# Output and down weights loaded in 4096-byte runs and put in row order on the chip, with a shorter root and a split silu

## The chip, the cores and the metric

The kernel runs on one core of a Trainium2 chip. The metric is the device time of one execution in microseconds (us). The engines are TensorE (PE; its weight loads are a row of their own, PEld), VectorE (DVE), ScalarE (ACT), GpSimd (POOL) and SyncE (SP), which here only issues transfers. Sixteen DMA engines move data between the chip's main memory and the on-chip memory SBUF (128 partitions); TensorE writes its sums to PSUM, eight banks of 512 f32 values in each partition.

## The reference

Two layers, each an attention block over a cached K and V and then a two-matrix silu block, for eight sequences of one token. The second layer uses the same caches and weights as the first.

```python
B, D = 8, 512;  Hq, Hkv, Sk, Dh = 32, 8, 8192, 128;  F = 1792      # all bf16
def A(x):                        # x: 8 x 512, after layernorm
    q = x @ wq                   # 512 x 4096
    p = softmax(q . K / sqrt(128))         # four query heads share one K/V head
    return (p . V) @ wo                    # wo: 4096 x 512
def Bl(x):
    return silu(x @ w1) @ w2               # w1: 512 x 1792, w2: 1792 x 512
for _ in range(2):
    x = x + A(layernorm(x))
    x = x + Bl(layernorm(x))
```

K and V are 8 x 8 x 8192 x 128 each, 134 MB each; the weights are 4.19 MB (wq), 4.19 MB (wo), 1.84 MB (w1) and 1.84 MB (w2).

## The kernel before

The unit of work is a chunk: 2048 keys of one sequence and one K/V head, 512 KB of K and 512 KB of V. Four chunks make a task (one sequence, one head, one layer), and there are 128 tasks. An arena of 28 slots of 512 KB in SBUF (`ARENA`, `NSLOT`) holds chunks. A planner (`lay_loads`, line 184) gives every load its slot, and the point at which that slot is free; `issue_until` (444) issues the loads in the planner's order on SP's queue as the program passes these points, so that SP waits in order for whoever last used the slot. The tasks are ordered so that parts of K and V read for the first layer are still in SBUF for the second.

For a chunk, TensorE transposes K in 16 blocks of 128x128 (line 479), ScalarE and VectorE copy the halves back from PSUM (485, 487), TensorE forms the scores with four 32-column tiles side by side (505), and six chunks later multiplies V by the probabilities (565). The softmax of a task is spread over VectorE, GpSimd and ScalarE (514 to 554). `LAG` is 6 chunks, `AHEAD` is 8.

When all heads of a sequence are through the first layer, its rest follows as a chain of small steps put between the chunks (`chain_of`, 715): the sum over wo (683, called from `add_heads`, 807), layernorm (`ln_stages`, 582, with the reciprocal root of line 632 on: a bit shift for a first guess, then two refinements), w1, tanh for silu, w2, layernorm, and the queries of the second layer. After the last task `closing` (776) does the end of the second layer for all eight sequences at once: layernorm, w1, silu (792 to 797) and w2 (799).

The start is written out by hand. SP issues eight K loads (456), then wq (449), then the first loads of all other slots (459), then wo, w1 and w2 (452 to 454). In wo_sb, partition p holds rows p, 128 + p, 256 + p and so on, so each piece that is read is one row of 512 values, 1024 bytes; w2 is the same, w1 is read in pieces of 3584 bytes, and a K or V load in pieces of 4096 bytes (8192 where two chunks go together). TensorE transposes the eight K chunks (840), multiplies by wq (843), and VectorE copies the queries to `QA` (844). Then the loop over the chunks begins (878).

Of the kernel before, what the change touches and what calls it, by code (L numbers as in the profile page):

```python
# [22 lines left out]
NTP = 3  # L23
# [215 lines left out]
def _build(ctx, nc, A_x, A_k_cache, A_v_cache, A_wq, A_wo, B_w1, B_w2, out):  # L239
# [50 lines left out]
    w1_sb = sb([128, KT, F], BF16, "w1")  # L290
    w2_sb = sb([128, FT, D], BF16, "w2")
    ident = sb([128, 128], BF16, "ident")
    XA = sb([128, 3, KT, B], BF16, "XA")
    XT = [XA[:, n] for n in range(3)]
    NT = 4
# [53 lines left out]

    syn = Sync(nc, ctx)  # L350
    slsem = [DmaCounter(syn.new_sem(f"sl{i}")) for i in range(NSLOT)]
    wsem = {n: DmaCounter(syn.new_sem(f"w_{n}")) for n in ("wq", "wo", "w1", "w2", "x")}
    osem = syn.new_sem("osem")

    R = {}
# [54 lines left out]
    with nc.Block() as block:  # L410

        @block.sync
        def _(sync_eng):
            dma(act, Xr[0:B, :], x_in, wsem["x"], writes=["P"])

            op(pool, lambda: pool.memset(ident[:, :], 0.0), writes=["ident"])
            along, down_ = QA[:, 0, :], QA[:, 1, :]
            op(dve, lambda: dve.memset(along[:, 0:1], 0.0), writes=["QA0"])
            n = 1
            while n < QR:  # L420
                op(dve, lambda n=n: dve.tensor_scalar(along[:, n:2 * n], along[:, 0:n], float(n), None, op0=ALU.add),
                   reads=["QA0"], writes=["QA0"])
                n *= 2
            op(dve, lambda: dve.transpose(down_, along), reads=["QA0"], writes=["QA1"])
            for t in range(NT):
                at = slice(t * QR, (t + 1) * QR)
                op(dve, lambda at=at: dve.tensor_tensor(ident[at, at], along[at, :], down_[at, :], ALU.is_equal),
                   reads=["QA0", "QA1", "ident"], writes=["ident"])
# [32 lines left out]

            evacs = [0]

# [118 lines left out]
            def ln_stages(xv, rx, n, bufs):  # L582
# [48 lines left out]

                def third():
                    vi, yi = v.bitcast(INT32), y.bitcast(INT32)
                    op(dve, lambda: dve.tensor_scalar(v, s1a[:, 0:n], 1.0 / D, LN_EPS, op0=ALU.mult, op1=ALU.add),
                       reads=["s1a"], writes=["vr"])
                    op(dve, lambda: dve.tensor_scalar(yi, vi, 1, None, op0=ALU.logical_shift_right),
                       reads=["vr"], writes=["yr"])
                    op(dve, lambda: dve.tensor_scalar(yi, yi, -1.0, RSQRT_SEED, op0=ALU.mult, op1=ALU.add),
                       reads=["yr"], writes=["yr"])
                    op(dve, lambda: dve.tensor_scalar(v, v, -0.5, None, op0=ALU.mult), reads=["vr"], writes=["vr"])  # L640
                    near(RSQRT_STEPS[0])

                def fourth():
# [20 lines left out]
            def wo_part(g, rhs_of, r_rhs, n, first, last):  # L664
                steps = []
                for o in range(KT):
                    for h in range(g * REP, (g + 1) * REP):
                        steps.append(
                            lambda o=o, h=h: pe.matmul(
                                MISC[:, o * n:(o + 1) * n], wo_sb[:, h, o * 128:(o + 1) * 128], rhs_of(h),  # L670
                                start=first and o == 0 and h == g * REP, stop=last and h == (g + 1) * REP - 1,
                                skip_group_check=True,
                            )
                        )
                mm_group(steps, reads=["wo"] + r_rhs, writes=["MISC"])

            def spread(col):
                return col.to_broadcast([128, QR])
# [36 lines left out]
            def chain_of(b):  # L715
# [21 lines left out]
                def down(q0, q1):  # L737
                    def run():
                        tiles([(t, hsT[:, q:q + 1], across(w2_sb[:, q, :], 0, KT)[:, t], q == 0, q == FT - 1)
                               for q in range(q0, q1) for t in range(NT)], ["w2", "hsT"])  # L740
                    return run

                AC = KB // QR
# [32 lines left out]
            def closing(n):  # L776
                xc, _sq, xn, _tag = ends
                memset = op(pool, lambda: pool.memset(ones, 1.0), writes=[r_half(spare, 0), r_half(spare, 1), "ones"])
                for r in ("xc8", "sq8", "xn8", "eh8", "th8", "hs8", "XF", "XO"):
                    syn.release(memset, writes=[res(r)])  # L780

                def rest():
                    x0, x1 = XT[2], XT[1]
                    add_residual(x1, "XT1", x0, "XT2", n)
                    centre, spread_of, guess, root = ln_stages(x1, "XT1", n, ends)
                    centre()
                    op(act, lambda: act.copy(xn, xc), reads=["xc8"], writes=["xn8"])
                    project(w1_sb, "w1", FT, KT, lambda k: xn[:, k, :], "xn8", n)
                    spread_of()
                    guess()  # L790
                    root()
                    op(dve, lambda: dve.scalar_tensor_tensor(
                        ehN.rearrange("p (f b) -> p f b", b=n), MISC[:, 0:FT * n].rearrange("p (f b) -> p f b", b=n), 0.5,
                        yr[:, 0:n].unsqueeze(1).to_broadcast([128, FT, n]), op0=ALU.mult, op1=ALU.mult),
                       reads=["MISC", "yr"], writes=["eh8"])
                    op(act, lambda: act.activation(thN, ehN, ACT.Tanh), reads=["eh8"], writes=["th8"])
                    op(dve, lambda: dve.scalar_tensor_tensor(hsN, thN, 1.0, ehN, op0=ALU.add, op1=ALU.mult),
                       reads=["th8", "eh8"], writes=["hs8"])
# [8 lines left out]
            def add_heads(b):  # L807
# [3 lines left out]
                if b < B:  # L811
                    a = at1[b % 3]
                    tiles([(t, a[:, h:h + 1], across(wo_sb[:, h, :], 0, KT)[:, t], first and h == g * REP,
                            last and h == (g + 1) * REP - 1)
                           for h in range(g * REP, (g + 1) * REP) for t in range(NT)], ["wo", f"at1_{b % 3}"])
# [28 lines left out]
            op(  # L844
                dve,
                lambda: dve.tensor_copy(
                    QA[:, :, :].rearrange("p b h -> p h b"),
                    MISC[:, 0:HQ * B].rearrange("p (h b) -> p h b", b=B)),
                reads=["MISC"], writes=[f"QA{b}" for b in range(B)],
            )  # L850

            emit_q(0)
# [106 lines left out]
```

## Time and profile before

| | |
|---|---|
| time, median of 3 runs | 1151.31 us (1146.54 to 1153.69) |
| profiled execution, its own time | 1151.22 us |
| its span, first to last instruction | 1149.4 us |
| mean granted TensorE clock | 0.910 |
| bytes by DMA | 459.43 MB in 100333 packets |
| wo, from issue to landing | 29.3 us |
| wq, from issue to landing | 19.7 us |

The profile gives for each engine its busy time, and for a stretch of time the busy time of each engine with its count of instructions, the granted TensorE clock (1.00 is full speed), the mean busy share of the DMA engines and GB/s. The share goes over 1 where packets overlap, so the GB/s say more than the share. A timeline row has start, length, engine, line, operation, what it writes and reads, its shapes and, in brackets, how long the engine stood idle before it and who ended that. A wait is given to the one that came last. The chain that ended last is followed back from the last instruction, at each step to what released it.

### The profile page before, as it was taken

The numbers are of one execution on the slowest core, as the hardware profiler recorded it, in microseconds if no ns is written. First come the engines' busy times: TensorE is split into PE (matmuls) and PEld (weight loads), VectorE is DVE, ScalarE is ACT, GpSimd is POOL, SyncE is SP. The second block draws the span as 40 slices with busy tenths as digits, with TensorE's granted clock in tenths as the row PEclk, the third lists the DMA queues.
The fourth block names the chain that finished last, engine by engine and source line by source line (L and its number), as shares of the span: only waits on it lengthen the run. The fifth ranks groups of instructions, "written<-read, shape, count | busy, mean of one in ns | idle before, by whom it ended". The sixth has DMA issues, their size and how long they took to land.

```text
span 1149.4 us, 42541 instructions
## 1 busy us (share of the span) xinstructions
PE 930.6 (81%) x18616; PEld 698.0 (61%) x18616; DVE 538.5 (47%) x1713; ACT 471.5 (41%) x747; POOL 117.6 (10%) x299
## 2 busy tenths in 40 slices
PE   5568888888888887888888887888878888888786
PEld 4356664666566664766566655666566655666565
DVE  3334453445534553446434553446434553456333
ACT  3235442455325541454235542554245432554332
POOL 0000011001110101001110111001100111011110
PEclk8689997899879997999789996999789996999897
DMA  9999999999999999999999999999999999999994
GB/s 371 393 396 414 383 386 412 418 411 387 406 418 416 394 402 419 418 410 393 400 418 416 389 407 417 419 404 378 413 419 414 390 410 417 417 400 399 404 418 190
DMA packets 100333, 459.43 MB, mean 400 GB/s; under 512 B 10540, under 2 KB 16436, under 8 KB 73780
## 3 DMA queue, kind: packets, MB, share of 16 engines
q1 hardware_dynamic: 100132, 456.70, 99.0%
q8 instruction: 147, 2.41, 0.9%
q14 instruction: 38, 0.31, 0.1%
q10 hardware_dynamic: 16, 0.01, 0.0%
HBM read 456.66 MB, written 0.01 MB: 397 GB/s over the span
## 4 chain that ended last, share of the span: by engine, by line
DMA 55%; PE 28%; DVE 10%; SPq 3%; issue 3%; ACT 0%; POOL 0%; POOLq 0%; ACTq 0%; DVEq 0%
DMA arena<-in_A_v_cache_dram 43%; PE TPp L479 15%; DMA arena<-in_A_k_cache_dram 10%; DVE arena L487 8%; PE SCp L505 6%; PE OTp L565 4%; SPq L379 3%; DMA wo<-in_A_wo_dram 3%; PE MISC L683 2%; PE TPp L545 1%; DVE small L554 0%; DVE small L535 0%; DVE small L525 0%; PE MISC L655 0%; ACT P L529 0%
## 5 line engine op out<-in xcount | busy, mean ns | idle before, releaser
L485 ACT COPY arena<-TPp 128x1024 bf16<-128x1024 bf16 x352 | 356.2, 1012 | 434.1 <-PE TPp L479 431.6
L487 DVE COPY arena<-TPp 128x1024 bf16<-128x1024 bf16 x352 | 243.4, 692 | 367.5 <-PE TPp L479 364.7
L479 PE MATMUL TPp<-ident,arena 128*128 128x128 bf16 x5632 | 391.6, 225 | 23.6 <-DMA arena<-in_A_k_cache_dram 20.9
L479 PEld LDWEIGHTS TPp<-ident,arena 128*128 128x128 bf16 x5632 | 330.0, 100 | 118.8 <-DMA arena<-in_A_k_cache_dram 65.9
L565 PE MATMUL OTp<-PT,arena 128*128 128x32 bf16 x8192 | 292.7, 179 | 74.7 <-DMA arena<-in_A_v_cache_dram 71.5
L565 PEld LDWEIGHTS OTp<-PT,arena 128*128 128x128 bf16 x8192 | 251.9, 98 | 158.9 <-DMA arena<-in_A_v_cache_dram 132.5
L505 PE MATMUL SCp<-arena,QB 128*32 128x512 bf16 x2048 | 223.9, 429 | 76.7 <-DVE arena L487 24.9
L529 ACT ACTIVATE P<-SCp,small 128x512 bf16<-128x512 f32 x128 | 88.0, 687 | 206.5 <-DVE small L527 148.6
L516 DVE TENSOR_REDUCE small<-SCp 128x1 f32<-128x512 f32 x128 | 88.5, 691 | 109.5 <-PE SCp L505 108.4
L505 PEld LDWEIGHTS SCp<-arena,QB 128*32 128x32 bf16 x2048 | 61.4, 97 | 118.3 <-ACT arena L485 64.8
L520 POOL PARTITION_ALL_REDUCE small<-small x128 | 47.6, 372 | 607.1 <-DVE small L518 607.1
L537 POOL PARTITION_ALL_REDUCE small<-small x128 | 55.4, 433 | 356.6 <-DVE at L579 160.9
L545 PE MATMUL TPp<-ident,P 128*128 128x128 bf16 x512 | 55.2, 237 | 11.5 <-ACT P L529 11.0
L535 DVE TENSOR_SCALAR small<-small 128x4 f32<-128x4 f32 x128 | 28.6, 223 | 37.9 <-ACT P L529 37.9
L549 DVE COPY PT<-TPp 128x256 bf16<-128x256 bf16 x128 | 36.7, 287 | 10.9 <-PE TPp L545 9.1
L545 PEld LDWEIGHTS TPp<-ident,P 128*128 128x128 bf16 x512 | 32.7, 103 | 14.7 <-ACT P L529 14.5
L683 PE MATMUL MISC<-wo,at 128*32 128x128 bf16 x1024 | 27.2, 239 | 13.1 <-DMA wo<-in_A_wo_dram 13.1
L518 DVE TENSOR_SCALAR small<-small 128x4 f32<-128x4 f32 x128 | 29.4, 229 | 4.5
L525 DVE TENSOR_TENSOR small<-small 128x4 f32<-128x4 f32 x128 | 19.9, 156 | 20.9 <-POOL small L520 20.9
L696 DVE STREAM_TRANSPOSE UP<-MISC 128x128 f32<-128x128 f32 (+2 forms) x40 | 22.1, 552 | 15.3 <-PE MISC L683 15.3
L683 PEld LDWEIGHTS MISC<-wo,at 128*32 128x32 bf16 x1024 | 16.3, 102 | 16.0 <-DMA wo<-in_A_wo_dram 13.2
L529 ACT ACTIVATION_READ_ACCUMULATOR P<-SCp,small 128x1 f32 x128 | 24.7, 193 | 0.0
(70 smaller groups left out, 230.0 us busy)
## 6 DMA issues: line engine op xcount, KB each, us to landing
arena<-in_A_v_cache_dram SPq DMA_DIRECT2D x133, 1024.0 KB, 14.5
arena<-in_A_v_cache_dram SPq DMA_DIRECT2D x230, 512.0 KB, 6.7
arena<-in_A_k_cache_dram SPq DMA_DIRECT2D x214, 512.0 KB, 7.2
arena<-in_A_k_cache_dram SPq DMA_DIRECT2D x69, 1024.0 KB, 20.5
wq<-in_A_wq_dram SPq DMA_DIRECT2D x1, 4096.0 KB, 19.7
wo<-in_A_wo_dram SPq DMA_DIRECT2D x1, 4096.0 KB, 29.3
w<-in_B_w_dram SPq DMA_DIRECT2D x2, 1792.0 KB, 24.8
P<-in_A_x_dram ACTq DMA_DIRECT2D x1, 8.0 KB
```

The costliest lines, as they stand in the source:

```text
L479: lambda c=c: pe.transpose(tpv[:, c, :], chunk(slot, h * GRP + c), ident[:, :])
L485: op(act, lambda: act.copy(dst, TPp[tb][:, :]), reads=[f"TP{tb}"], writes=[r_half(slot, h)])
L487: op(dve, lambda: dve.tensor_copy(dst, TPp[tb][:, :]), reads=[f"TP{tb}"], writes=[r_half(slot, h)])
L505: lambda t=t: pe.matmul(SCp[bank][t * QR:(t + 1) * QR, :], QB[qn][:, NGRAN - 1 - k:NGRAN - 1 - k + QR], keys[:, t * KB:(t + 1) * KB], star ...
L516: op(dve, lambda: dve.tensor_reduce(mxp[st][:, :], SCp[bank][:, :], AX.X, ALU.max), reads=[f"SC{bank}"], writes=[f"mxp{st}"])
L520: op(pool, lambda: pool.partition_all_reduce(mxa[st][:, :], mxr[st][:, :], 128, bass.bass_isa.ReduceOp.max), reads=[f"mxr{st}"], writes=[f ...
L529: op(act, lambda: act.activation(P[:, :], SCp[bank][:, :], ACT.Exp, bias=nb[st][:, 0:1], scale=SM_SCALE, accum_out=rs[st][:, :]), reads=[f ...
L537: op(pool, lambda: pool.partition_all_reduce(ssa[st][:, :], ssm[st][:, :], 128, bass.bass_isa.ReduceOp.add), reads=[f"ssm{st}"], writes=[f ...
L545: lambda c=c: pe.transpose(tpv[:, c, :], P[:, c * 128:(c + 1) * 128], ident[:, :])
L549: op(dve, lambda: dve.tensor_copy(PT[:, :, :, :], tpv.rearrange("p c (t q) -> p c t q", q=QR)[:, :, :, 0:NGRAN * REP]), reads=[f"TP{tb}"], ...
L565: lambda n=n, cc=cc: pe.matmul(otp, chunk(slot, n), PT[:, cc % CPB, (cc // CPB) % NT, cc // (CPB * NT)::NGRAN].unsqueeze(2).to_broadcast([ ...
L683: lambda t=t, col=col, w=w, start=start, stop=stop: pe.matmul(MISC[t * QR:(t + 1) * QR, 0:math.prod(w.shape[1:])], spread(col), w, start=s ...
```

## The change

Three parts.

First, wo and the first 12 of w2's 14 blocks of 128 rows are read in 11 loads of 512 KB: partition p receives rows 4p to 4p + 3 of a group of 512 rows, 4096 bytes in one piece. They go to slots 17 to 27, which no K or V load has used yet, and are issued behind the eight K loads and ahead of wq. TensorE then puts the rows in the order that the rest of the kernel expects. A matrix `place` of ones and zeros, 32 rows in each of four 32-row tiles, with a one in every fourth column, sends row 4p + i of tile t to partition 4(p mod 32) + i of bank t: four matmuls (i = 0 to 3) add up in each of four PSUM banks, each using 32 rows of the array. ScalarE copies two of the banks to wo_sb or w2_sb, VectorE the other two. Groups alternate between two sets of four banks. `lay_runs` stands behind the transposes of the first eight K chunks and ahead of the product with wq. The first K and V loads of slots 17 to 27 now wait for their group's matmuls; w1 and the last two blocks of w2 are issued behind them. The waits of the users of wo and w2 name single blocks.

Second, the first guess of the reciprocal root takes -0.5 v in place of v, so that the shift and the scaling of v fall away: four VectorE operations become two, in each of the 18 calls.

Third, in `closing` the silu is cut in two halves of seven blocks, and the w2 product in two groups of 28 matmuls, the first of which needs only the first half.

```diff
-RSQRT_SEED = float(0x5F376908)
+RSQRT_SEED = float(0x5F376908 - (1 << 30) - (1 << 22))
...
+            place = QA[:, 2:7, :].rearrange("p b h -> p (b h)")[:, 0:RUN - 1 + 128]
+            op(pool, lambda: pool.memset(place, 0.0), writes=["place"])
...
+            op(dve, lambda: dve.tensor_tensor(place[:, RUN - 1:RUN - 1 + 128:RUN], along, down_, ALU.is_equal),
+               reads=["QA0", "QA1", "place"], writes=["place"])
...
             def load_rest():
-                dma(sp, wo_sb[:, :, :], A_wo.rearrange("(h p) d -> p h d", p=128), wsem["wo"], writes=["wo"])
                 dma(sp, w1_sb[:, :, :], B_w1.rearrange("(kt p) f -> p kt f", p=128), wsem["w1"], writes=["w1"])
-                dma(sp, w2_sb[:, :, :], B_w2.rearrange("(ft p) d -> p ft d", p=128), wsem["w2"], writes=["w2"])
+                dma(sp, w2_sb[:, FT - FT % RUN:, :], B_w2[(FT - FT % RUN) * 128:, :].rearrange("(ft p) d -> p ft d", p=128),
+                    wsem["w2"], writes=["w2"])
+
+            runs = [(A_wo, wo_sb, "wo", g) for g in range(HQ // RUN)] + [(B_w2, w2_sb, "w2", g) for g in range(FT // RUN)]
+            lent = list(range(NSLOT - len(runs), NSLOT))
+
+            def load_runs():
+                for (w, _to, _name, g), s in zip(runs, lent):
+                    dma(sp, ARENA[:, s * SLOT:(s + 1) * SLOT],
+                        w[g * RUN * 128:(g + 1) * RUN * 128, :].rearrange("(p i) d -> p (i d)", i=RUN), slsem[s],
+                        writes=[r_half(s, h) for h in range(HALVES)])
 
             for _n in range(AHEAD):
                 issue(queue.pop(0))
+            load_runs()
             load_wq()
-            issue_until(-2)
-            load_rest()
...
+            def lay_runs():
+                wide = [(SCp[0], "SC0"), (SCp[1], "SC1"), (OTp, "OT"), (UP, "UP")]
+                wide2 = [(TPp[n][:, :].bitcast(FP32), f"TP{n}") for n in range(NTP)] + [(MISC, "MISC")]
+                for n, ((_w, to, name, g), s) in enumerate(zip(runs, lent)):
+                    banks = wide if n % 2 == 0 else wide2
+                    mm_group(
+                        [
+                            lambda t=t, i=i: pe.matmul(
+                                banks[t][0][:, 0:D], place[t * QR:(t + 1) * QR, RUN - 1 - i:RUN - 1 - i + 128],
+                                ARENA[t * QR:(t + 1) * QR, s * SLOT + i * D:s * SLOT + (i + 1) * D],
+                                start=(i == 0), stop=(i == RUN - 1), tile_position=(t * QR, 0),
+                            )
+                            for i in range(RUN) for t in range(NT)
+                        ],
+                        reads=[r_half(s, h) for h in range(HALVES)] + ["place"], writes=[r for _b, r in banks],
+                    )
+                    for t in range(NT):
+                        bank, r = banks[t]
+                        if t % 2 == 0:
+                            op(act, lambda: act.copy(to[:, g * RUN + t, :], bank[:, 0:D]), reads=[r], writes=[f"{name}{g * RUN + t}"])
+                        else:
+                            op(dve, lambda: dve.tensor_copy(to[:, g * RUN + t, :], bank[:, 0:D]),
+                               reads=[r], writes=[f"{name}{g * RUN + t}"])
...
-                    op(dve, lambda: dve.tensor_scalar(v, s1a[:, 0:n], 1.0 / D, LN_EPS, op0=ALU.mult, op1=ALU.add),
+                    op(dve, lambda: dve.tensor_scalar(v, s1a[:, 0:n], -0.5 / D, -0.5 * LN_EPS, op0=ALU.mult, op1=ALU.add),
                        reads=["s1a"], writes=["vr"])
-                    op(dve, lambda: dve.tensor_scalar(yi, vi, 1, None, op0=ALU.logical_shift_right),
+                    op(dve, lambda: dve.tensor_scalar(yi, vi, -0.5, RSQRT_SEED, op0=ALU.mult, op1=ALU.add),
                        reads=["vr"], writes=["yr"])
-                    op(dve, lambda: dve.tensor_scalar(yi, yi, -1.0, RSQRT_SEED, op0=ALU.mult, op1=ALU.add),
-                       reads=["yr"], writes=["yr"])
-                    op(dve, lambda: dve.tensor_scalar(v, v, -0.5, None, op0=ALU.mult), reads=["vr"], writes=["vr"])
...
-                    op(act, lambda: act.activation(thN, ehN, ACT.Tanh), reads=["eh8"], writes=["th8"])
...
-                    project(w2_sb, "w2", KT, FT, lambda k: hsN[:, k * n:(k + 1) * n], "hs8", n)
+                    parts = [(f, slice(f * n, (f + FT // 2) * n)) for f in range(0, FT, FT // 2)]
+                    for f, at in parts:
...
+                        op(act, lambda at=at: act.activation(thN[:, at], ehN[:, at], ACT.Tanh),
+                           reads=[f"eh8{f}"], writes=[f"th8{f}"])
...
             for c in range(AHEAD):
                 for h in range(HALVES):
                     emit_t(c, h)
+            lay_runs()
+            issue_until(-2)
+            load_rest()
             project(wq_sb, "wq", HQ, KT, lambda k: opens[2][:, k, :], "PT", B)
```

More of the change, by code (lines that the diff above doesn't have):

```diff
@@ L292, in _build @@
     ident = sb([128, 128], BF16, "ident")
+    RUN = 4
+    assert RUN * D == SLOT and HQ % RUN == 0
     XA = sb([128, 3, KT, B], BF16, "XA")
@@ L674, in wo_part @@
                         )
-                mm_group(steps, reads=["wo"] + r_rhs, writes=["MISC"])
+                mm_group(steps, reads=[f"wo{h}" for h in range(g * REP, (g + 1) * REP)] + r_rhs, writes=["MISC"])
             def spread(col):
@@ L791, in rest @@
                     root()
[L792 to L798, printed above, removed]
@@ new lines, in rest @@
+                    for f, at in parts:
+                        op(dve, lambda at=at: dve.scalar_tensor_tensor(
+                            hsN[:, at], thN[:, at], 1.0, ehN[:, at], op0=ALU.add, op1=ALU.mult),
+                           reads=[f"th8{f}", f"eh8{f}"], writes=[f"hs8{f}"])
+                    for f, _at in parts:
+                        mm_group(
+                            [
+                                lambda o=o, k=k: pe.matmul(
+                                    MISC[:, o * n:(o + 1) * n], w2_sb[:, k, o * 128:(o + 1) * 128],
+                                    hsN[:, k * n:(k + 1) * n], start=(k == 0 and o == 0), stop=(k == FT - 1),
+                                    skip_group_check=True,
+                                )
+                                for k in range(f, f + FT // 2) for o in range(KT)
+                            ],
+                            reads=all_of("w2") + [f"hs8{f}"], writes=["MISC"],
+                        )
@@ L848, in _ @@
                     MISC[:, 0:HQ * B].rearrange("p (h b) -> p h b", b=B)),
-                reads=["MISC"], writes=[f"QA{b}" for b in range(B)],
+                reads=["MISC"], writes=[f"QA{b}" for b in range(B)] + ["place"],
             )
```

14 lines of the change are left out of this document (10 added, 4 removed).

## The prediction

> **What bounds the kernel now.** I read the page first (busy shares, the 40 slices, the packets, the chain that ended last), then busy time by stretches of the first 80 us, then the timeline of the start and of the end, and last the waits of TensorE.
>
> ```profile
> span 1149.4 us, 42541 instructions
> ...
> PE 930.6 (81%) x18616; PEld 698.0 (61%) x18616; DVE 538.5 (47%) x1713; ACT 471.5 (41%) x747; POOL 117.6 (10%) x299
> ...
> DMA  9999999999999999999999999999999999999994
> ...
> DMA packets 100333, 459.43 MB, mean 400 GB/s; under 512 B 10540, under 2 KB 16436, under 8 KB 73780
> ...
> DMA 55%; PE 28%; DVE 10%; SPq 3%; issue 3%; ACT 0%; POOL 0%; POOLq 0%; ACTq 0%; DVEq 0%
> ```
>
> The 16 DMA engines are busy in every slice but the last, no compute engine is above 81%, and 55% of the chain is DMA. So bytes and the rate at which they come set the time, and a microsecond of transfer saved early moves all that follows, if the engines that free the slots keep up. 459 MB at 400 GB/s is the whole span. Where is the rate low at the start?
>
> ```profile
> 0.00:10.00 10.00, 5.45 (x52) 5.13 (x53) 6.15 (x32) 3.85 (x4) 1.35 (x9) 1.00 0.80 282
> 10.00:20.00 10.00, 5.60 (x83) 4.74 (x81) 4.15 (x6) 5.43 (x6) 0.00 (x0) 1.00 1.02 425
> 20.00:30.00 10.00, 3.58 (x128) 3.49 (x128) 1.27 (x1) 0.15 (x2) 0.00 (x0) 0.54 1.01 411
> 30.00:40.00 10.00, 7.67 (x100) 4.47 (x100) 3.46 (x11) 2.02 (x6) 1.19 (x3) 0.50 1.02 412
> 40.00:50.00 10.00, 7.85 (x148) 6.37 (x148) 4.62 (x15) 5.08 (x8) 0.80 (x2) 0.94 1.02 405
> 50.00:60.00 10.00, 0.00 (x0) 0.00 (x0) 0.00 (x0) 0.62 (x2) 0.00 (x0) 0.57 1.10 350
> 60.00:70.00 10.00, 7.34 (x144) 6.02 (x144) 2.15 (x7) 2.75 (x3) 0.43 (x1) 0.74 1.07 374
> ```
> ```profile
> 52.00:60.00 8.00, 0.00 (x0) 0.00 (x0) 0.00 (x0) 0.00 (x0) 0.00 (x0) 0.50 1.10 349
> ...
> 62.00:64.00 2.00, 1.73 (x28) 1.21 (x29) 0.00 (x0) 0.00 (x0) 0.00 (x0) 0.50 1.04 410
> ...
> 66.00:70.00 4.00, 3.85 (x88) 3.20 (x88) 1.31 (x5) 1.74 (x2) 0.43 (x1) 1.00 1.10 351
> ```
>
> The last three columns are TensorE's granted clock, the DMA share and GB/s. The queue of SP is in order: 8 K slots, wq, 20 more slots, wo, w1, w2. At 512 KB a slot the bytes ahead of wo are 28 x 0.524 + 4.19 = 18.9 MB, and the rows of 10 us add up to that at about 49 us; wo's 4.19 MB then cover 49 to 61, w1's 1.84 MB 61 to 65, w2's 1.84 MB 65 to 70.4, where 26.7 MB are in. So 349 GB/s is wo (1024-byte runs), 410 is w1 (3584-byte runs) and 351 is w2 (1024-byte runs again). TensorE idles in the first, works in the last, and idles in part of the 411 stretch, so its work isn't the cause; the run length goes with the rate.
>
> **The change, part by part.**
>
> *Loads.* wo (4.19 MB) and 12 of w2's 14 blocks (1.57 MB) go from 1024-byte to 4096-byte runs, the shape of a K slot load. Loads of at least that length ran at 425, 411 and 412 GB/s from 10 to 40 us, 416 on the mean. So 5.77 MB take 13.9 us in place of 16.5 at 349: 2.6 us less. Bounds: 2.5 us at the lowest such row (411), 2.9 at the highest (425); I take 2.6. The last 0.26 MB of w2 stay at 351. The Trainium skill, DMA: Bandwidth & Descriptors, Specifications, puts the least transfer for line rate at 512 bytes, by which 1024-byte runs lose nothing and this term is 0; the same page (Why small descriptors are slow) counts some 3 extra cycles for each packet of 32-byte beats, which by 35/32 against 131/128 would give an estimate of 388 GB/s and 1.0 us. This trace, with 349 beside 410 (w1) and 416, disagrees with both.
>
> *SP's order.* SP now issues 8 K, 11 runs, wq, 9 slots without a wait, and then the first loads of slots 17 to 27, each behind a wait for the group that empties that slot; w1 and the rest of w2 come behind these. No byte is added. wq is moved behind 11 x 0.524 = 5.8 MB.
>
> ```profile
> 24.94 3.58 PE L655 MATMUL MISC<-PT,wq 128*128 128x8 bf16 x128 [9.09 <-DMA wq<-in_A_wq_dram]
> ...
> 28.55 1.27 DVE L846 CAST QA<-MISC 128x256 bf16<-128x256 f32 x1 [11.97 <-PE MISC L655]
> ...
> 30.10 2.75 PE L505 MATMUL SCp<-arena,QB 128*32 128x512 bf16 x24 [1.59 <-ACT QB L496]
> ...
> 48.66 0.56 PE L565 MATMUL OTp<-PT,arena 128*128 128x32 bf16 x16
> ...
> 62.27 0.62 PE L683 MATMUL MISC<-wo,at 128*32 128x128 bf16 x16 [13.06 <-DMA wo<-in_A_wo_dram]
> ```
> ```profile
> PE OTp L565 <- DMA arena<-in_A_v_cache_dram: 7.0, 8, 2.6
> ```
>
> The first rows are the start of the timeline, the last one is TensorE's largest wait between 70 and 130 us (total, times, longest). By the rows, 8.4 MB (K and wq) were in at 23.2 us and wq was used at 24.9, a lag of 1.7. With the runs ahead, 14.2 MB are in at 37.2, so wq is used at 38.9: 14 us later, and the scores begin at 44 instead of 30. What that costs: in the kernel before, TensorE did its first steps from 30.1 to 49.2 and then stood 13 us for wo. Now wo lies in SBUF by then, so the same steps end at 63.2 and the work that began at 62.3 begins at 63.2. The transfers reach the 26.7 MB mark at 67.8 instead of 70.4. Measured against the data, TensorE is 0.9 + 2.6 = 3.5 us later than before; the 7.0 us that it waited for V between 70 and 130 cover that, so I charge nothing. Without that cover it is 2.6 us, the whole gain. V and K loads for slots 0 to 7 wait for the first eight scores, done by about 50, while the transfers need them at 68.
>
> *Laying the rows out.* 11 groups, each 16 matmuls on four 32-row tiles (4 passes of 512 columns if the four overlap), then two copies on ScalarE and two on VectorE from 128x512 f32 in PSUM.
>
> ```profile
> L529 ACT ACTIVATE P<-SCp,small 128x512 bf16<-128x512 f32 x128 | 88.0, 687 | 206.5 <-DVE small L527 148.6
> L516 DVE TENSOR_REDUCE small<-SCp 128x1 f32<-128x512 f32 x128 | 88.5, 691 | 109.5 <-PE SCp L505 108.4
> ```
> ```profile
> 0.73 0.20 POOL L416 MEMSET ident<- 128x128 bf16 x1 [0.29 <-POOLq L944]
> ...
> 2.16 0.77 DVE L427 TENSOR_TENSOR ident<-QA 32x32 bf16<-32x32 bf16 x4
> ...
> 4.58 3.59 PE L479 MATMUL TPp<-ident,arena 128*128 128x128 bf16 x32 [1.26 <-DMA arena<-in_A_k_cache_dram]
> ...
> 15.89 0.69 DVE L487 COPY arena<-TPp 128x1024 bf16<-128x1024 bf16 x1 [0.38 <-PE TPp L479]
> ```
>
> The 24 score matmuls at 30.10 are 6 passes of four column tiles in 2.75 us at clock 0.50, 0.46 each. A group is then 4 x 0.46 = 1.8 us at half clock and about half of that at full clock, if row tiles overlap as column tiles do; copies of 0.69 make 1.4 us for each engine, beside the next group's matmuls on the other four banks. The bounds are 0.9 us for a group and, with no overlap at half clock, 16 x 0.46 = 7.3; I take 1.8, since the same array runs four column tiles at once. Groups start when the eight K chunks are out (16.6 us by the last row) and the last run lands at 28.7. They end at 16.6 + 11 x 1.8 + 1.4 = 37.8 at worst, ahead of wq at 38.9. Nothing is charged: TensorE, VectorE and ScalarE stood idle there, and the cover is gone above (38.9 - 16.6) / 11 = 2.0 us for a group. The transfers come to slot 17 at about 49 us, when all groups are done, so SP's new waits hold nothing up. The memset of the place matrix on GpSimd (0.2 us as that of ident) and its compare on VectorE (0.77 / 4, 0.2 us) put ident 0.2 us later, while the first transposes wait 1.3 us for K.
>
> *Root two operations fewer; silu in halves.* In the closing part both are on the path.
>
> ```profile
> 1140.73 0.19 DVE L595 SCALAR_TENSOR_TENSOR arena<-SCp,XA 128x32 f32<-128x32 f32 x1 [0.43 <-PE SCp L605]
> ...
> 1142.34 0.17 DVE L638 TENSOR_SCALAR small<-small 128x8 int32<-128x8 int32 x1
> 1142.42 0.16 DVE L640 TENSOR_SCALAR small<-small 128x8 f32<-128x8 f32 x1
> 1142.55 0.17 DVE L627 TENSOR_TENSOR small<-small 128x8 f32<-128x8 f32 x1
> ...
> 1143.82 0.28 DVE L792 SCALAR_TENSOR_TENSOR arena<-MISC,small 128x112 f32<-128x112 f32 x1
> 1144.12 0.30 ACT L796 ACTIVATE arena<-arena 128x112 f32<-128x112 f32 x1 [2.95 <-DVE arena L792]
> 1144.45 0.28 DVE L797 SCALAR_TENSOR_TENSOR arena<-arena 128x112 bf16<-128x112 f32 x1 [0.36 <-ACT arena L796]
> 1144.79 1.65 PE L655 MATMUL MISC<-arena,w 128*128 128x8 bf16 x56 [1.90 <-DVE arena L797]
> ```
> ```profile
> L638 DVE TENSOR_SCALAR small<-small x18: 153/153/172, 5.9 to 1142.3; 128x1 int32<-128x1 int32 x16, 128x8 int32<-128x8 int32 x2
> ...
> L640 DVE TENSOR_SCALAR small<-small x18: 143/144/164, 6.0 to 1142.4; 128x1 f32<-128x1 f32 x16, 128x8 f32<-128x8 f32 x2
> ```
>
> Without L638 and L640 the step at 1142.55 starts at 1142.34: 0.2 us. Halves of 56 elements cost between the 32-element 0.19 and the 112-element 0.28, say 0.22, in each of three steps of 0.28 to 0.30: 0.2 us earlier for the first matmul. The second half's sums run beside the first 28 matmuls (0.8 us), so they hide; were they late, the 0.2 is lost (0 to 0.3). In the 16 root calls of the eight sequences 16 x (0.153 + 0.144) = 4.8 us of VectorE go; nobody's wait names these lines and VectorE is at 47%, so I take 0, with 4.8 us as the other bound.
>
> **The sum.** The profiled execution took 1151.2 us (span 1149.4, 1.8 around it), within 0.1 us of the median 1151.3 of the three runs shown (1146.5 to 1153.7). 1151.2 - 2.6 - 0.2 - 0.2 = 1148.2 us.
>
> **Rivals.** *The early gain is not kept* (1150.8): the low rate had another cause than the run length, or TensorE's 3.5 us of lag eat it. For it: TensorE at 81% has little room to catch up, and slots it frees late are filled late. Against it: 410 for w1 between 349 and 351, and 7.0 us of waits for V. The 512-byte rule of the page named above leads to this outcome; the trace is against it.
>
> *VectorE's shorter roots count in every sequence* (1148.2 - 4.8 = 1143.4): for it, each of the eight sequences has a stretch with more VectorE work and a lower rate, as the second of the next rows shows beside the first (the third busy time is VectorE's, the last column GB/s); against it, no wait on those lines.
>
> ```profile
> 240.00:250.00 10.00, 8.65 (x194) 7.24 (x194) 4.70 (x13) 5.68 (x8) 0.80 (x2) 1.00 1.02 415
> ...
> 270.00:280.00 10.00, 8.60 (x168) 6.32 (x160) 6.75 (x27) 4.93 (x7) 1.62 (x4) 1.00 0.99 366
> ```
>
> *The four row tiles run one after the other* (slower). A group is then 16 passes: 3.7 us at full clock, 7.3 at half. Up to 2.0 us for a group wq's landing covers it, and to 2.0 + (7.0 - 3.5) / 11 = 2.3 the waits for V; from there each further microsecond costs 11. That gives 1148.2 + 11 x 1.4 = 1163.6 at full clock and 1203 at half. For it: no row here has a row tile, and row tiles write all 128 partitions of four banks at once, where column tiles write 32 each. Against it: the six passes above overlap four ways on this array. The Trainium skill, TensorE: Matmul & The Clock Gate, Measured speedup vs the span model, has 3.07 for four row tiles of 512 columns; no run here shows it, and an estimate by it is 16 x 0.46 / 3.07 = 2.4 us for a group at half clock and 1.2 at full.
>
> **How the numbers follow.** Forecast 0.66, gain not kept 0.15, roots count 0.10, row tiles in series 0.09. About 1% (11.5 us) is what a measurement of this kernel can tell from no change. Only the serial case is past it on the slow side: slower 0.09. Faster by over 1% needs the root case with a run scatter of 4 us more: 0.02. Within 1%: 0.89. The forecast's own range, with the scatter of the runs, is 1145 to 1151; the range reaches from the root case, 1143.4, to the case of no gain with the 2.4 us by which the highest run lies above the median: 1143.4 to 1153.2. It leaves out the serial case and the fringes, under 2 in 10.
>
> **What would show it.** Right: packets under 2 KB fall by 5632 less some 160, no stretch at 350 GB/s longer than 1 us before 70 us, the 26.7 MB in by 68; groups of at most 2 us, the last copy done before wq's first matmul near 39; no wait for wo; the end from root to last matmul 0.4 us shorter. Wrong: a rate below 410 in the runs' 14 to 28 us, groups above 2.3 us, a DMA share below 1 at 48 to 70, or TensorE without waits for V from 70 to 130.

## The result and the profile after

| | before | after |
|---|---|---|
| median, first comparison (22 runs each) | 1147.39 us | 1143.66 us |
| ratio, first comparison | | 0.9963, 95% interval 0.9945 to 0.9981 |
| median, second comparison (35 and 12 runs) | 1147.12 us | 1146.76 us |
| ratio, second comparison | | 0.9991, 95% interval 0.997 to 1.0013 |
| profiled execution, span | 1149.4 us | 1138.3 us |
| second profile of each, span | 1144.8 us | 1141.2 us |

Ratios are those of mean times; the first leaves out one slow run of the changed kernel (1158.93 us). The second comparison was taken with the last experiments and shares no run with the first. The changed kernel is faster by 4.2 us (2.2 to 6.3) in the first and by 1.0 us (from 3.4 faster to 1.5 slower) in the second. The sum forecast a ratio of 1148.2 / 1151.2 = 0.9974, which both intervals hold.

The page of the changed kernel:

```profile
span 1138.3 us, 42936 instructions
...
PE 934.8 (82%) x18792; PEld 695.4 (61%) x18792; DVE 549.9 (48%) x1702; ACT 483.4 (42%) x770; POOL 117.5 (10%) x300
...
DMA  9999999999999999999999999999999999999995
...
DMA packets 96270, 459.45 MB, mean 404 GB/s; under 512 B 10700, under 2 KB 10964, under 8 KB 69716
...
DMA 55%; PE 29%; DVE 11%; issue 3%; SPq 2%; ACT 0%; POOL 0%; POOLq 0%; ACTq 0%; DVEq 0%
```

The bytes are the same, and packets under 2 KB fell from 16436 to 10964, which is 5632 less 160. Bytes still bound the kernel. The stretches of the start, in the same columns as before (clock, DMA share and GB/s last):

```profile
0.00:10.00 10.00, 5.68 (x60) 5.28 (x60) 6.39 (x32) 4.10 (x4) 1.49 (x10) 1.00 0.82 286
10.00:20.00 10.00, 8.01 (x122) 5.03 (x120) 6.37 (x10) 7.33 (x10) 0.00 (x0) 1.00 1.02 412
20.00:30.00 10.00, 8.21 (x128) 2.60 (x128) 9.99 (x16) 8.59 (x16) 0.00 (x0) 1.00 1.03 414
30.00:40.00 10.00, 1.09 (x40) 0.96 (x36) 1.47 (x3) 1.07 (x2) 0.00 (x0) 0.65 1.01 416
40.00:50.00 10.00, 6.48 (x132) 3.79 (x129) 3.11 (x8) 1.16 (x5) 0.82 (x2) 0.50 1.03 410
50.00:60.00 10.00, 8.70 (x164) 7.17 (x161) 3.70 (x11) 3.81 (x5) 0.80 (x2) 0.83 1.02 415
60.00:70.00 10.00, 8.97 (x204) 7.34 (x201) 4.92 (x13) 5.76 (x8) 0.80 (x2) 1.00 1.03 405
```

The rows of 350 and 374 GB/s are gone; 415 and 405 stand in their place, and the long pieces themselves came in at 412 GB/s (14 to 28 us). VectorE is the busy engine between 20 and 30 us (9.99 of 10): the layout runs at the pace of its copies. Its last copy ends at 31.5. Parts of the timeline of the same kernel (start, length, engine, line, operation):

```profile
15.48 0.39 PE L486 MATMUL SCp<-arena,QA 32*128 32x512 bf16 x2 [0.21 <-DMA arena<-in_A_wo_dram]
15.49 0.39 PE L486 MATMUL OTp<-arena,QA 32*128 32x512 bf16 x1
15.49 0.39 PE L486 MATMUL UP<-arena,QA 32*128 32x512 bf16 x1
15.71 0.38 PE L486 MATMUL SCp<-arena,QA 32*128 32x512 bf16 x2
...
16.14 0.38 PE L486 MATMUL SCp<-arena,QA 32*128 32x512 bf16 x2
...
25.09 0.69 DVE L500 CAST wo<-SCp 128x512 bf16<-128x512 f32 x1
...
39.04 3.58 PE L693 MATMUL MISC<-PT,wq 128*128 128x8 bf16 x128 [8.91 <-DMA wq<-in_A_wq_dram]
...
44.21 2.75 PE L546 MATMUL SCp<-arena,QB 128*32 128x512 bf16 x24 [1.59 <-ACT QB L537]
...
63.01 0.41 PE L721 MATMUL MISC<-wo,at 128*32 128x128 bf16 x16
```
```profile
PE OTp L606 <- DMA arena<-in_A_v_cache_dram: 4.7, 6, 1.6
```

Four row tiles start within 0.01 us of each other, passes follow every 0.22 us, and a group's 16 matmuls are out in about 1.0 us at full clock. wq is used at 39.04 (38.9 in the prediction), the scores begin at 44.21 (44), the step over wo at 63.01 without a wait (63.2). TensorE's waits for V between 70 and 130 us, the last row, fell from 7.0 to 4.7 us. At the end, first one row of the kernel before and then the changed kernel:

```profile
1141.93 0.17 DVE L634 TENSOR_SCALAR small<-small 128x8 f32<-128x8 f32 x1 [0.54 <-POOL small L618]
```
```profile
1131.20 0.17 DVE L675 TENSOR_SCALAR small<-small 128x8 f32<-128x8 f32 x1 [0.54 <-POOL small L659]
...
1131.61 0.17 DVE L668 TENSOR_TENSOR small<-small 128x8 f32<-128x8 f32 x1
...
1133.13 0.39 ACT L836 ACTIVATE arena<-arena 128x56 f32<-128x56 f32 x2 [2.68 <-DVE arena L832]
...
1133.68 1.66 PE L845 MATMUL MISC<-arena,w 128*128 128x8 bf16 x56 [1.52 <-DVE arena L839]
```

From the root's first operation to the first w2 matmul it is 2.48 us in the changed kernel. Before it was 2.86 (1141.93 to 1144.79), so 0.38 us went.

How much of the loads' gain is kept? One row for the first 110 us of each kernel, before and after:

```profile
0.00:110.00 110.00, 67.88 (x1252) 54.48 (x1253) 38.71 (x116) 38.69 (x54) 6.98 (x23) 0.83 1.01 393
```
```profile
0.00:110.00 110.00, 79.03 (x1466) 57.83 (x1467) 53.18 (x138) 50.83 (x77) 7.12 (x24) 0.89 1.00 402
```

9 GB/s over 110 us are 0.99 MB, 2.4 us at 413 GB/s. 0.04 MB of that is an earlier first transfer (286 against 282 in the first row), which leaves 2.3 us. With the 0.4 us of the end that makes 2.7 us. The two spans differ by 11.1 us, so some 8 us of the difference between these two profiles lie behind 110 us, where up to the closing part only the roots work otherwise than before. Two of the experiments ask what they are.

### The profile page after: what moved, and what is told of

It is laid out like the page before. It is cut to its first block, busy times and chain, and to the rows that moved or that the text cites. A ratio compares the mean times of both kernels' runs of the same rounds, so it can differ in the third digit from the quotient of the medians.

```text
span 1138.3 us, 42936 instructions
## 1 busy us (share of the span) xinstructions
PE 934.8 (82%) x18792; PEld 695.4 (61%) x18792; DVE 549.9 (48%) x1702; ACT 483.4 (42%) x770; POOL 117.5 (10%) x300
## 2 busy tenths in 40 slices
DMA packets 96270, 459.45 MB, mean 404 GB/s; under 512 B 10700, under 2 KB 10964, under 8 KB 69716
## 4 chain that ended last, share of the span: by engine, by line
DMA 55%; PE 29%; DVE 11%; issue 3%; SPq 2%; ACT 0%; POOL 0%; POOLq 0%; ACTq 0%; DVEq 0%
DMA arena<-in_A_v_cache_dram 42%; PE TPp L520 15%; DMA arena<-in_A_k_cache_dram 11%; DVE arena L528 9%; PE SCp L546 7%; PE OTp L606 4%; DMA wq<-in_A_wq_dram 2%; PE MISC L721 2%; SPq L381 1%; PE TPp L586 1%; DVE small L595 0%; DVE small L576 0%; PE MISC L693 0%; ACT P L570 0%; DVE small L566 0%
## 5 line engine op out<-in xcount | busy, mean ns | idle before, releaser
L520 PE MATMUL TPp<-ident,arena 128*128 128x128 bf16 x5632 | 386.6, 223 | 23.1 <-DMA arena<-in_A_k_cache_dram 20.0
L520 PEld LDWEIGHTS TPp<-ident,arena 128*128 128x128 bf16 x5632 | 325.4, 100 | 116.5 <-DMA arena<-in_A_k_cache_dram 64.9
L568 DVE TENSOR_REDUCE small<-small 128x1 f32<-128x4 f32 x128 | 20.1, 157 | 4.4
```

Of the source, the lines that this page charges most:

```text
L520: lambda c=c: pe.transpose(tpv[:, c, :], chunk(slot, h * GRP + c), ident[:, :])
```

## The experiments

The four theories are those of the prediction: the pieces' length sets the rate and the gain is kept; the gain isn't kept; the roots count in every sequence; the layout has a price.

**Loads and layout alone.** The root and the closing part are those of the kernel before.

```diff
-RSQRT_SEED = float(0x5F376908 - (1 << 30) - (1 << 22))
+RSQRT_SEED = float(0x5F376908)
...
-                    parts = [(f, slice(f * n, (f + FT // 2) * n)) for f in range(0, FT, FT // 2)]
...
```

> The weights in 4096-byte runs and their rows laid out by TensorE, with the old root and the silu in one piece. Theory A (the gain is the shorter transfers): 2.3 to 2.6 us less than before, ratio about 0.998; the 10 us rows show no stretch near 350 GB/s ahead of 70 us, and the closing part, from the first root operation to the first matmul of the last product, takes 2.86 us as before. Rival B (the shorter roots carry most of it in every sequence): 1 us or less, ratio above 0.999.

Ratio 0.998 (0.9957 to 1.0002). The size is that of the loads' 2.3 us, but the interval reaches no change. The end, from the root's first operation to the first w2 matmul, takes 2.86 us as in the kernel before.

**Root and silu alone.** The kernel before with the second and third part of the change.

```diff
-RSQRT_SEED = float(0x5F376908)
+RSQRT_SEED = float(0x5F376908 - (1 << 30) - (1 << 22))
...
```

> The loads as before, with the new root and the silu in halves. Theory A: 0.4 us less than before, all of it in the closing part, 2.48 us in place of 2.86; ratio 0.9997, not to be told from 1. Rival B: 2 to 5 us less, ratio 0.996 to 0.998, with less time in each of the eight stretches in which a sequence goes to the second layer.

Ratio 1.001 (0.9991 to 1.0028). Removing 32 VectorE operations from the sequences brings nothing that shows: the 4.8 us of the second rival would be 0.996, which the interval excludes. The end takes 2.49 us, so its 0.4 us come from these two parts.

**Tiles listed one after the other.**

```diff
-                            for i in range(RUN) for t in range(NT)
+                            for t in range(NT) for i in range(RUN)
```

> The changed kernel, but the four matmuls of a 32-row tile come one after another, then the next tile's, so that passes hardly overlap: the trace of the changed kernel has 0.22 us for a pass, so a group goes from 1.0 us to 2.9 to 3.5. By the prediction's working a group above 2.3 us costs 11 us for each further one: 7 to 13 us slower than the changed kernel, ratio to before 1.002 to 1.008. Rival C (TensorE has more room to catch up than the 7 us of waits for V): no more than 2 us slower than the changed kernel, ratio below 0.998.

Ratio 0.9971 (0.9948 to 0.9993). The edit didn't make what it was meant to make. The timeline of this kernel:

```profile
15.31 0.40 PE L486 MATMUL SCp<-arena,QA 32*128 32x512 bf16 x2 [0.21 <-DMA arena<-in_A_wo_dram]
15.34 0.39 PE L486 MATMUL OTp<-arena,QA 32*128 32x512 bf16 x1
15.35 0.39 PE L486 MATMUL UP<-arena,QA 32*128 32x512 bf16 x1
15.54 0.39 PE L486 MATMUL SCp<-arena,QA 32*128 32x512 bf16 x2
```

Though four matmuls of one tile now stand ahead of the next tile's first, all four tiles still start within 0.04 us and go on every 0.2 us. So it says nothing on the price of a layout in series, and the next two kernels were made for that.

**The layout done three and four times over.** Each group's matmuls are repeated, with the same result (`range(4)`, and `range(3)` in the second kernel).

```diff
-                            for i in range(RUN) for t in range(NT)
+                            for _again in range(4) for i in range(RUN) for t in range(NT)
```

> The changed kernel with the 16 matmuls of each group done four times over (each time from the start, so the rows come out the same): a group takes 64 x 0.22 / 4 = 3.5 us of passes and some 3.9 us with its waits, so the last one ends near 58 us and the queries are made 19 to 20 us later than in the changed kernel. By the prediction's working everything above 2.3 us for a group costs 11 times as much: (3.9 - 2.3) x 11 = 17 us more than the changed kernel, ratio to before about 1.011. Rival C (TensorE catches up because the loads keep coming from slots that are free anyway): up to 5 us more than the changed kernel, ratio at most 1.001.

> The changed kernel with each group's 16 matmuls done three times over (the result is the same). A group is then 2.6 us (with four times it was 3.46), the layout ends at about 44, the queries' product starts at 43.5 to 44 in place of 39.0. By the prediction's working, with the cover ending at 2.3 us for a group, (2.6 - 2.3) x 11 = 3.3 us are lost: ratio to the kernel before 0.999 to 1.000. By the run with four times, where the start was 13.9 us late and the transfers lost 8.0 us by 130 us, the cover is 5.9 us and 4.7 us of lag cost nothing: 0.9963, and the rates at 100 to 130 us stay above 370 GB/s.

Four times: ratio 1.0031 (1.0002 to 1.0059), 0.0068 or 7.8 us above the changed kernel's first ratio, 0.0040 or 4.6 us above its second. Three times: 0.9992 (0.997 to 1.0014). The prediction's working put it at 0.999 to 1.000, but the changed kernel itself has 0.9991 in the same comparison, so this ratio shows no loss. The timelines of the scores, three times and then four times:

```profile
44.37 3.35 PE L693 MATMUL MISC<-PT,wq 128*128 128x8 bf16 x128
...
49.32 2.75 PE L546 MATMUL SCp<-arena,QB 128*32 128x512 bf16 x24 [1.59 <-ACT QB L537]
```
```profile
52.98 3.36 PE L693 MATMUL MISC<-PT,wq 128*128 128x8 bf16 x128
...
57.92 2.75 PE L546 MATMUL SCp<-arena,QB 128*32 128x512 bf16 x24 [1.59 <-ACT QB L537]
```

wq no longer ends the wait (no bracket): the layout does. The scores are 5.1 and 13.7 us later than the 44.21 of the changed kernel. Where it is lost, by stretches, three times and then four times:

```profile
100.00:110.00 10.00, 8.49 (x188) 6.74 (x177) 4.67 (x14) 4.99 (x8) 0.80 (x2) 1.00 1.03 414
110.00:120.00 10.00, 8.31 (x173) 7.03 (x171) 4.41 (x13) 5.38 (x8) 0.80 (x2) 1.00 1.02 401
120.00:130.00 10.00, 8.42 (x198) 6.93 (x194) 5.92 (x18) 5.58 (x9) 1.20 (x3) 1.00 1.01 390
```
```profile
100.00:110.00 10.00, 8.64 (x181) 7.05 (x178) 4.39 (x12) 4.95 (x8) 0.80 (x2) 1.00 0.77 300
110.00:120.00 10.00, 8.52 (x187) 7.04 (x184) 4.87 (x13) 5.82 (x9) 0.80 (x2) 1.00 0.78 275
120.00:130.00 10.00, 7.95 (x156) 6.47 (x157) 4.69 (x14) 5.11 (x9) 0.80 (x2) 1.00 0.92 282
```

With three times there is no loss up to 130 us. With four times the DMA share drops to 0.77 from 100 us on: the transfers stand for slots that TensorE hasn't freed. 414 + 401 + 390 less 300 + 275 + 282 GB/s are 3.48 MB or 8.4 us by 130 us. But the losses grow behind 130 us, as the first 200 us show (the changed kernel, three times, four times):

```profile
0.00:200.00 200.00, 154.46 (x2941) 111.09 (x2942) 98.62 (x285) 85.89 (x136) 17.91 (x51) 0.90 1.01 403
```
```profile
0.00:200.00 200.00, 165.98 (x3284) 118.17 (x3284) 97.93 (x284) 85.97 (x136) 17.52 (x50) 0.95 1.01 400
```
```profile
0.00:200.00 200.00, 169.52 (x3312) 118.25 (x3312) 94.69 (x271) 84.20 (x131) 16.29 (x47) 0.95 0.98 383
```

By the bytes in the table further below, three times over is 0.55 to 0.79 MB or 1.3 to 1.9 us behind the two profiles of the changed kernel at 200 us, and four times over 4.05 to 4.29 MB or 9.8 to 10.4 us. So of the lags of 5.1 and 13.7 us, 3.2 to 3.8 and 3.3 to 3.9 us cost nothing, about the 3.5 us that the prediction had as the cover beyond wq's landing. TensorE's waits for V are gone from 70 to 130 us in both. These are single profiles; the ratios, with intervals of 2 to 3 us to either side, show less of a loss.

**wq ahead of the runs.** The queries are computed before the layout.

```diff
-            load_runs()
             load_wq()
+            load_runs()
...
```

> The changed kernel with wq ahead of the runs again: the queries are made before the rows are laid out, so the scores start about 40 us instead of 44; the place matrix is put in P, since QA now holds queries. Theory A: TensorE's later start is covered, so the time is the changed kernel's within 1 us, ratio about 0.996. Rival C (the later start eats part of the gain): 1 to 4 us less than the changed kernel, ratio 0.993 to 0.995.

Ratio 0.997 (0.995 to 0.9991), the changed kernel's within the interval. Moving wq behind 5.8 MB costs nothing that shows, as the prediction had it.

**Other lengths of piece, without the layout.** These start from the kernel before. Where pieces are longer than a row, the step that puts rows in order is left out, so wo and w2 hold their rows permuted. The first reads wo and 12 blocks of w2 in 4096-byte pieces, the second the same with w2 in one load of 7168-byte pieces, the third wo in 2048-byte pieces, the fourth wo in two loads of 512-byte pieces (the rows in order).

```diff
-dma(sp, wo_sb[:, :, :], A_wo.rearrange("(h p) d -> p h d", p=128), ...)
+dma(sp, wo_sb[:, :, :].rearrange("p (g i) d -> p g (i d)", i=4), A_wo.rearrange("(g p i) d -> p g (i d)", p=128, i=4), ...)
...
```

> The kernel before, with wo and 12 blocks of w2 read in 4096-byte runs straight into their places; the step that puts the rows in order is left out, so the weights' rows are permuted. Theory A (length of the run sets the rate): wo's stretch goes from 349 to 405 to 415 GB/s, TensorE's wait for wo from 13.1 to about 11 us, ratio 0.998. Rival D (the low rate belongs to this place in the stream or to these tensors): the stretch stays near 350, ratio 1.000.

> The kernel before with wo read in 4096-byte pieces and w2 in one load of 7168-byte pieces straight into their places; the step that puts the rows in order is left out, so wo and w2 hold their rows permuted. The earlier version with w2 in two loads stood still for 4 us, because the second load waited on SP for the first to land; one load takes that wait away. Length of the pieces (A): wo and w2 at 405 to 420 GB/s, 26.7 MB in 2.5 to 3 us earlier than in the kernel before, and no stretch below 380 GB/s at 60 to 80 us; ratio 0.9975 to 0.998, near 0.996 if the same work is saved as in the changed kernel. Gain not kept (B): TensorE uses wo at 61.5, hardly earlier than at 62.3, and has to free the slots that the transfers reach 2.6 us earlier, so the transfers stand for that long: 0.9995 to 1.0005.

> The kernel before, with wo alone read in 2048-byte runs straight into its place (two rows a partition; rows permuted, the ordering step left out). Theory A with a fixed time for each piece, fitted to 1024 bytes at 351 and 4096 at 410 GB/s over 16 engines (46.7 and 160 ns for a piece, so 9 ns and 27 GB/s an engine): 388 GB/s for wo. Rival D: 350. Rival E (a threshold between 1024 and 2048 bytes): 410.

> The kernel before, with wo read in two loads of 512-byte pieces, rows in order. Theory A with the fixed time for each piece: 28 ns for a piece, 295 GB/s for wo, 2.2 us longer than the kernel before. Rival D: 350, no longer. Rival F (a piece below some length takes the same time whatever its length): 175 GB/s, 12 us longer.

The rate while wo comes in, in the order 4096, 2048 and 512 bytes:

```profile
50.00:60.00 10.00, 0.00 (x0) 0.00 (x0) 0.00 (x0) 0.00 (x0) 0.00 (x0) 0.53 1.02 407
...
68.00:70.00 2.00, 1.85 (x48) 1.45 (x45) 0.62 (x2) 0.39 (x2) 0.00 (x0) 1.00 0.09 37
```
```profile
54.00:56.00 2.00, 0.00 (x0) 0.00 (x0) 0.00 (x0) 0.00 (x0) 0.00 (x0) 0.50 1.05 387
```
```profile
52.00:54.00 2.00, 0.00 (x0) 0.00 (x0) 0.00 (x0) 0.00 (x0) 0.00 (x0) 0.50 1.16 294
```

With 1024 bytes at 349, the rate rises with the length alone: 294, 349, 387, 407. (With 4096 bytes the rows of 2 us swing from 399 to 418, so the row of 10 us stands for them.) This settles what the low rate came from. As times the two first kernels say less. With 4096 bytes the ratio is 0.9989 (0.9961 to 1.0016), but the row of 37 GB/s shows a stop of the edit's own making: it reads w2 in two loads, and the waits of SP's queue show what the second one waited for (total, times, longest):

```profile
SPq L379 <- DMA w<-in_B_w_dram: 17.1, 1, 17.1
```

One load of w2 takes that stop away:

```profile
50.00:60.00 10.00, 0.00 (x0) 0.00 (x0) 0.00 (x0) 0.00 (x0) 0.00 (x0) 0.65 1.02 407
60.00:70.00 10.00, 8.46 (x144) 6.77 (x144) 2.51 (x7) 3.06 (x4) 0.43 (x1) 0.66 1.03 417
70.00:80.00 10.00, 7.72 (x164) 6.29 (x164) 4.15 (x13) 4.68 (x7) 0.80 (x2) 1.00 1.01 417
```

The transfers don't stand at 60 to 80 us, so the reason given for a lost gain is not there; yet its ratio is 1.0004 (0.9984 to 1.0025), which misses 0.998 by a little. The kernels with 2048 and 512 bytes ran once each, with spans of 1148.1 and 1151.8 us; the scatter of the runs hides what the lengths cost there. The second load of 512-byte pieces also waited for the first (23.0 us on SP's queue, 12 GB/s at 56 to 58 us), so the 294 GB/s are the rate ahead of a stop.

**Both kernels once more, unchanged.**

> The kernel before once more, unchanged. If the profile of the kernel before is one draw of a scatter, the row of 314 GB/s at 140 to 150 us doesn't come back (360 to 410), the median over the runs lies at 1147 to 1149 and not at the profile's own 1151.2, and the ratio is 1.000 with an interval of about 0.002 to either side. If 1151.2 is its true level: the row comes back, and the median is 1150 to 1152.

> The changed kernel once more, unchanged. If the changed kernel's gain is the 2.3 us of loads and 0.4 us of the end: ratio 0.9976 with an interval that reaches 0.9963. If there is a further gain of about 1.5 us that no row of the first 70 us shows: 0.9963 again or below, and the profile is again ahead of the kernel before in the stretches at 260 to 290 and 390 to 410 us. Its first 110 us move 48.3 MB as in the first profile, and the span may lie anywhere from 1138 to 1147.

The kernel before: median 1147.56, ratio 1.0003 (0.9985 to 1.002). The changed kernel: 1146.76, ratio 0.9991 (0.997 to 1.0013). The stretches of the kernel before where its two profiles part, first profile and then the second:

```profile
130.00:140.00 10.00, 7.74 (x128) 5.55 (x128) 6.03 (x25) 3.92 (x6) 1.62 (x4) 0.84 0.99 378
140.00:150.00 10.00, 8.87 (x212) 6.90 (x204) 5.72 (x17) 5.11 (x8) 0.95 (x3) 0.99 0.93 314
```
```profile
130.00:140.00 10.00, 8.26 (x156) 5.85 (x144) 6.71 (x26) 4.93 (x7) 1.61 (x4) 1.00 0.97 363
140.00:150.00 10.00, 8.64 (x204) 6.73 (x204) 5.61 (x20) 4.33 (x8) 1.59 (x4) 1.00 1.01 372
```

The row of 314 GB/s doesn't come back. (372 - 314 - 378 + 363) x 10 us are 0.43 MB, 1.0 us of the 4.6 us between the two spans. The dips at the changes of sequence differ from one execution of a kernel to the next. Over its first 110 us the second profile of each shows the same gain, the kernel before and then the changed one:

```profile
0.00:110.00 110.00, 67.46 (x1249) 54.02 (x1250) 38.94 (x117) 38.90 (x54) 6.96 (x23) 0.83 1.01 395
```
```profile
0.00:110.00 110.00, 77.26 (x1468) 56.02 (x1469) 53.01 (x138) 50.91 (x77) 7.10 (x24) 0.92 1.00 402
```

7 GB/s over 110 us are 0.77 MB, and 0.19 MB is to be added because here the kernel before began earlier (310 against 291 GB/s in its first 10 us): 0.96 MB, 2.3 us once more. (The 48.3 MB that were expected are those of the first 120 us.)

One profile of each kernel can also be followed further: the MB that had come in by a given time, less those of the first 10 us, so that an earlier begin doesn't count.

| | 110 us | 200 us | 400 us | 1000 us |
|---|---|---|---|---|
| before, two profiles | 40.42, 40.39 | 75.88, 75.93 | 157.49, 157.85 | 402.20, 403.29 |
| root and silu alone | 40.40 | 76.63 | 158.11 | 402.45 |
| changed, two profiles | 41.40, 41.36 | 77.82, 77.58 | 159.64, 159.47 | 405.58, 405.34 |
| loads and layout alone | 41.38 | 77.72 | 159.57 | 402.59 |
| tiles listed in series | 41.38 | 77.78 | 159.31 | 405.40 |
| wq ahead of the runs | 41.35 | 77.68 | 159.45 | 403.49 |
| straight 7168 | 41.46 | 77.79 | 159.51 | 401.80 |
| layout three times | 41.29 | 77.03 | 158.84 | 404.42 |
| layout four times | 40.20 | 73.53 | 154.75 | 400.07 |

Against the three profiles with the old loads, every kernel of the table with long pieces and no added work is ahead by 0.9 to 1.1 MB at 110 us and by 1.2 to 2.2 MB, 2.9 to 5.2 us, at 400 us. So the early gain is still there and has grown; what adds to it isn't shown. By 1000 us the profiles part by more than that: wq ahead of the runs has lost 1.9 MB to the changed kernel since 400 us, and two kernels with long pieces have no lead left.

## Why the prediction was right or wrong

*What bounds it, and the loads.* Right in the rate: length sets it, in four lengths, and the term of 2.6 us measured 2.3 at 110 us in two pairs of profiles. The prediction has no term for the lead's growth up to 400 us. By the Trainium skill, DMA: Bandwidth & Descriptors, Specifications, 512 bytes are enough for line rate: this case disagrees, as 512-byte pieces ran at 294 GB/s and 1024-byte pieces at 349. The estimate of 388 GB/s that the prediction made from the same page for 1024 bytes (its fractions give 389) is reached at 2048 (387).

*wq, SP's order, TensorE's lag.* Right to 0.2 us for wq, the scores and the step over wo, and no stretch up to 70 us shows a loss. The cover of 3.5 us beyond wq's landing is borne out by the two kernels with a longer layout (3.2 to 3.9 us at 200 us, one profile each). The serial rival's price of (group - 2.3) x 11 us is 12.8 us for the 3.46 us of four times over; the trace gave some 10 at 200 us and the comparisons 4.6 to 7.8. Part of the excess is the start: the first group of that kernel began at 14.9 us, where the working had 16.6.

*The layout's price.* The bound held, the rate was better. The 1.8 us for a group rested on half clock; the granted clock was 1.00 from 10 to 30 us, a group's matmuls took about 1.0 us, and VectorE's two copies of 0.69, some 1.3 us for a group, set the pace. The end at 31.5 instead of 37.8 changed no time, as wq came at 39. The rival of tiles in series is out: they overlap. The Trainium skill's 3.07 for four row tiles (TensorE: Matmul & The Clock Gate, Measured speedup vs the span model) gave an estimate of 1.2 us at full clock; this trace is a little better, with four passes of 0.22 us.

*Root and silu.* 0.38 us of the forecast's 0.4, on the path of the end; nothing that shows in the sequences. The rival that gave these 4.8 us is out for the kernel with the old loads.

*The step that failed* is the base of the sum: "The profiled execution took 1151.2 us [...], within 0.1 us of the median 1151.3 of the three runs shown". The three runs are the first of the 22, whose median is 1147.4; in the other comparisons the kernel before has medians of 1147.1 to 1149.5. So the base stands some 2 to 4 us too high, about as much as the whole change is worth. Against 1147.4 the forecast of 1148.2 says no gain, while the first comparison excludes that; and 1143.66 lies at the low end of the range for this reason, not because the root rival came true. From 1147.4 the same terms give 1144.4, and with the measured ones 1144.7. With the base went the statement that 1% can be told from no change: 22 runs of each told 0.4%.

*What stays open.* The measured terms add up to 2.7 us, a ratio of 0.9976, which both comparisons hold. The five comparisons of kernels with long pieces put in order and no added work read 0.9963, 0.998, 0.9971, 0.997 and 0.9991, and three of their intervals exclude 1: a gain is shown, its size not closely. Whether the first comparison's further 1.5 us are real can't be settled: the lead at 400 us has room for them, the repetition doesn't have them. That the kernel with straight 7168-byte loads shows no gain in its time, though its transfers don't stand and its lead at 400 us is that of the others, is open too. So is whether the roots count once the loads are early: the two kernels with long pieces and the old root are the ones without a lead at 1000 us, but the ratio of loads alone (0.998) tells nothing of it, and no run was made for this.

## What to carry to other kernels

A kernel bound by bytes can gain from longer pieces where its loads are short, and row tiles of TensorE can put the rows in order at next to no time, as long as the layout ends before the data that come behind it. Size such a cover by making the added work longer until the rate of the transfers breaks, and look for the break where slots are used again (here at 100 us, 50 us behind the cause), and further on: three times over lost its 1.3 to 1.9 us only behind 130 us. Do the sum as a ratio and take its base from many runs: where runs scatter by 10 us, three of them can be off by as much as a change of 3 us.

## What the runs showed of the hardware

The time of a piece on one of the 16 engines, taken as always at work, follows a straight line: 294, 349, 387 and 407 GB/s are 27.9, 46.9, 84.7 and 161.0 ns for 512, 1024, 2048 and 4096 bytes. That is 0.037 ns for a byte and about 9 ns for each piece whatever its length, a fifth of the time of a 1024-byte piece and some 6% of that of a 4096-byte piece.

Matmuls on the four row tiles overlapped in both orders that were run: with four matmuls of one tile listed ahead of the next tile's, all four tiles started within 0.04 us.
